# Decoding float64 weights without a limit from below: the scale moves into the ScalarE pass

## The chip, the cores and the metric

One core of one Trainium2 chip. The metric is the device time of one execution in microseconds (us). "VectorE", "ScalarE", "GpSimd", "TensorE" and "SyncE" are the core's engines; the profile writes DVE, ACT, POOL, PE and SP for them, and PEld for TensorE's weight loads. In a line of the profile, `L231` is the line of the kernel's file that issued the instruction. The same instruction has another line number in each variant of the kernel; names and shapes identify it.

## The reference

An attention block over 8 batches whose output feeds a feed-forward block:

```python
scores = scale * x @ state.T;  xread = softmax(scores) @ state
scores2 = scale * state @ x.T; sread = softmax(scores2) @ x
x = concat([xread, sread])            # 4352 rows of 512
h = x @ w_in                          # 512 x 2048
out = (h * cos(h)) @ w_out            # 2048 x 512, float32 result
```

The two weight matrices arrive as float64, because a float32 array was multiplied by a float64 scalar. The kernel computes in float32, and no engine here is given float64: it builds the float32 from the two 32-bit words of each float64.

## The kernel before

The weights come in 20 loads, mostly 128 x 1024 values each (four of the first are 128 x 512; the last two repeat part of `w_out` near the end). Each load passes through the steps below: `1` and `2` on ScalarE, `a`, `b` and `c` on VectorE (`a` of load 1 on GpSimd), and a last add on GpSimd.

```python
def convert_part(i, p):
    ...
    if p == "1":        # high word, read as a float32, without its sign
        nc.scalar.activation(dst, raw.bitcast(F32)[:, :, :, 1], func=ACTF.Abs)
    elif p == "2":      # low word -> a float32 whose lowest bits are 0 to 8
        nc.scalar.activation(e, raw.bitcast(U32)[:, :, :, 0],
                             func=ACTF.Copy, scale=2.0 ** -51, bias=2.0)
    elif p == "a":      # the limit from below
        engine = nc.gpsimd if i == 1 else nc.vector
        engine.tensor_scalar(dst, dst, 2.0 ** -15, None, op0=ALU.max)
    elif p == "b":      # shift left by 3
        nc.vector.tensor_scalar(bits, bits, 3, None, op0=ALU.logical_shift_left)
    elif p == "c":      # put the sign back
        nc.vector.scalar_tensor_tensor(out=bits, in0=raw[:, :, :, 1],
                                       scalar=-2 ** 31, in1=bits, ...)
    else:               # add the low word's part
        nc.gpsimd.tensor_tensor(bits, bits, e.bitcast(I32), op=ALU.add)
```

A float64 has 11 exponent bits and a float32 has 8. Read as a float32, the high word has the upper 8 of the 11 as its exponent and the lower 3 at the top of its fraction, so a shift by 3 brings them into place. What is left over must vanish: the float64 bias is 896 larger than the float32 one, and 896 / 8 = 112. The kernel before lets the shift and the low words' leading bits (from the bias of 2.0) take care of it, with a limit from below for tiny values.

The work is cut into steps of one tile of 128 hidden features. In each step TensorE makes a hidden product (`h`), ScalarE rounds it (`q<-h`), VectorE subtracts (`q<-q,h`, "the gate's subtraction"), ScalarE takes Abs and sine, VectorE multiplies (`g_all<-h,q`, "the gate product"), and some steps later TensorE multiplies by `w_out`. `h` has two buffers: the hidden product of a step needs the gate product of two steps earlier. In steps 0 to 14, step 9 left out, each step also converts one load. Idle matmuls of zeros (`warm(n, to)`) fill a few known holes.

## Time and profile before

| | before |
|---|---|
| time, median of 3 | 792.2 us (791.26 to 793.64) |
| span of the profiled run | 789.4 us |
| TensorE busy | 767.3 us, 97% |
| VectorE busy | 431.2 us, 55% |
| ScalarE busy | 389.3 us, 49% |
| conversions | 18 loads before 112 us, 2 at 724 to 752 us |

A share averaged over 789 us hides that the first 112 us are another regime than the rest. There VectorE and ScalarE convert weights beside the gates, and TensorE waits for them. After that TensorE is the limit.

### The profile page before, as it was taken

Reading aid. Unit: us, or ns where it says so; the run is one execution under the profiler, and the core shown is the slowest. Engines: PE = TensorE matmul, PEld = TensorE weight load, DVE = VectorE, ACT = ScalarE, POOL = GpSimd, SP = SyncE. Lnnn points to the kernel's source line nnn. Section 1 sums busy time; section 2 is a strip of 40 time slices with the busy share of each in tenths; the row PEclk is TensorE's granted clock in tenths of the full one; section 3 lists DMA queues with packets and bytes.
Section 4 is the critical chain, followed back from the end, with each engine's and each line's share of the span. In section 5 each row is a group of like instructions: output and inputs, shape, how many; then the busy total and the mean of one; then the engine's idle time right before and its main releaser. Section 6 shows DMA issues by size and latency. Waiting matters only on the chain.

```text
span 789.4 us, 7555 instructions
## 1 busy us (share of the span) xinstructions
PE 767.3 (97%) x2664; PEld 340.4 (43%) x2664; DVE 431.2 (55%) x675; ACT 389.3 (49%) x626; POOL 178.7 (23%) x119
## 2 busy tenths in 40 slices
PE   8998999899999999999999999999999999999997
PEld 3442333344344344444444434434444444455554
DVE  5879887732564467744554467635553545431531
ACT  3877964644364445643473446443563445322222
POOL 3343359684000000551000000740000004610200
PEclk9999999999999999999999999999999999999999
DMA  8485461051010610150003410340100114000021
GB/s 239 160 248 179 127 140 28 0 90 18 0 27 14 107 27 14 30 104 0 15 14 54 80 27 7 53 75 0 27 1 0 27 27 117 17 0 15 14 41 40
DMA packets 161957, 43.49 MB, mean 55 GB/s; under 512 B 153920, under 2 KB 153920, under 8 KB 161920
## 3 DMA queue, kind: packets, MB, share of 16 engines
q1 hardware_dynamic: 161024, 42.49, 24.7%
q10 hardware_dynamic: 768, 0.39, 0.2%
q8 instruction: 21, 0.34, 0.2%
q0 software_dynamic: 128, 0.13, 0.1%
q14 instruction: 16, 0.13, 0.1%
HBM read 34.08 MB, written 8.91 MB: 54 GB/s over the span
## 4 chain that ended last, share of the span: by engine, by line
PE 80%; ACT 9%; DVE 8%; issue 1%; DMA 1%; POOL 1%; SPq 0%; DVEq 0%; POOLq 0%
PE o L534 44%; PE h L469 26%; PE at L316 4%; PE o L654 3%; PE at L406 2%; DVE q L478 1%; ACT q L483 1%; ACT q L484 1%; DVE g_all L490 1%; ACT s L227 1%; ACT q L475 1%; DVE xT L336 1%; ACT xT L362 1%; DVE aT L383 1%; PE o L316 1%
## 5 line engine op out<-in xcount | busy, mean ns | idle before, releaser
L469 PE MATMUL h<-aT,sw 128*128 128x512 f32 x512 | 243.2, 598 | 10.8 <-DVE g_all L490 10.2
L534 PE MATMUL o<-g_all,w_out 128*128 128x512 f32 x512 | 236.4, 598 | 1.1 <-POOL w_out L241 1.1
L496 POOL TENSOR_TENSOR g_all<-g_all 128x512 f32<-128x512 f32 x80 | 112.1, 1424 | 450.8 <-DVE g_all L490 447.2
L475 ACT ACTIVATE q<-h 128x512 f32<-128x512 f32 (+1 forms) x144 | 82.2, 571 | 261.7 <-PE h L469 261.6
L478 DVE SCALAR_TENSOR_TENSOR q<-q,h 128x512 f32<-128x512 f32 (+1 forms) x144 | 94.2, 654 | 207.3 <-ACT q L475 207.3
L534 PE MATMUL o<-g_all,s 128*128 128x512 f32 x384 | 177.3, 598 | 0.0
L490 DVE TENSOR_TENSOR g_all<-h,q 128x512 f32<-128x512 f32 (+1 forms) x144 | 94.8, 658 | 123.9 <-ACT q L484 117.7
L469 PEld LDWEIGHTS h<-aT,sw 128*128 128x128 f32 x512 | 96.8, 191 | 136.2 <-issue 110.2
L534 PEld LDWEIGHTS o<-g_all,w_out 128*128 128x128 f32 x512 | 94.0, 190 | 125.5 <-issue 118.4
L483 ACT ACTIVATE q<-q 128x512 f32<-128x512 f32 (+1 forms) x144 | 87.6, 608 | 96.3 <-DVE q L478 96.3
L534 PEld LDWEIGHTS o<-g_all,s 128*128 128x128 f32 x384 | 70.9, 190 | 91.7 <-issue 87.3
L484 ACT ACTIVATE q<-q,halfpi 128x512 f32<-128x512 f32 (+1 forms) x144 | 100.5, 698 | 4.5
L241 POOL TENSOR_TENSOR w_out<-w_out,s 128x1024 int32<-128x1024 int32 x10 | 23.9, 2389 | 79.4 <-DVE w_out L236 79.4
L496 DVE TENSOR_TENSOR g_all<-g_all 128x512 f32<-128x512 f32 x48 | 33.2, 692 | 1.6
L443 ACT COPY sw<-at 128x512 f32<-128x512 f32 x50 | 26.8, 589 | 9.0 <-PE at L316 9.0
L469 PE MATMUL h<-sT,w_in 128*128 128x256 f32 x128 | 30.2, 379 | 0.0
L654 PE MATMUL o<-w_out,g_all 128*128 128x512 f32 x64 | 29.6, 592 | 0.0
L469 PEld LDWEIGHTS h<-sT,w_in 128*128 128x128 f32 x128 | 24.3, 190 | 10.1 <-issue 6.2
L316 PE MATMUL at<-w_in,stT 64*32 64x512 f32 x400 | 27.2, 601 | 0.0
L241 POOL TENSOR_TENSOR w_in<-w_in,s 128x1024 int32<-128x1024 int32 (+1 forms) x10 | 19.7, 1966 | 32.1 <-DVE w_in L236 18.6
L540 DVE SCALAR_TENSOR_TENSOR held<-o,held 128x512 f32<-128x512 f32 x40 | 25.3, 676 | 2.3 <-PE o L534 2.3
L561 DVE STREAM_TRANSPOSE ot<-held 128x512 f32<-128x512 f32 x32 | 22.2, 692 | 0.0
(83 smaller groups left out, 443.5 us busy)
## 6 DMA issues: line engine op xcount, KB each, us to landing
out_dram<-ot SPq DMA_DIRECT2D x132, 64.0 KB, 2.0
g_all<-in_moe_w_out_dram SPq DMA_DIRECT2D x8, 1024.0 KB, 4.9
g_all<-in_moe_w_in_dram SPq DMA_DIRECT2D x6, 1024.0 KB, 5.2
xT<-in_x_dram SPq DMA_DIRECT2D x96, 64.0 KB, 2.3
x_b<-in_x_dram SPq DMA_DIRECT2D x24, 256.0 KB, 4.7
x_b<-in_x_dram SPq DMA_DIRECT2D x16, 128.0 KB, 3.9
g_all<-in_moe_w_in_dram SPq DMA_DIRECT2D x4, 512.0 KB, 6.0
x_b<-in_moe_w_out_dram SPq DMA_DIRECT2D x1, 1024.0 KB, 6.1
```

Of the source, the lines that this page charges most:

```text
L241: nc.gpsimd.tensor_tensor(bits, bits, e.bitcast(I32), op=ALU.add)
L316: nc.tensor.matmul(out=(to or at)[j][Ns * k:Ns * k + Ns, 0:n], lhsT=w[D * j:D * j + D, self.b, Ns * k:Ns * k + Ns], rhs=r(slice(D * j, D * ...
L443: (copy or nc.scalar.copy)(sw_of[self.b, nt][:, j, c0:c1], to[j][:, 0:c1 - c0])
L469: nc.tensor.matmul(out=t.hp, lhsT=t.lhs(i), rhs=t.rhs(i), start=(i == 0), stop=(i == t.kn - 1))
L475: nc.scalar.activation(t.q, t.hp, func=ACTF.Copy, bias=MAGIC)
L478: nc.vector.scalar_tensor_tensor(out=t.q, in0=t.q, scalar=MAGIC, in1=t.hp, op0=ALU.subtract, op1=ALU.subtract)
L483: nc.scalar.activation(t.q, t.q, func=ACTF.Abs)
L484: nc.scalar.activation(t.q, t.q, func=ACTF.Sin, bias=halfpi, scale=-TWO_PI)
L490: nc.vector.tensor_tensor(t.g, t.hp, t.q, op=ALU.mult)
L496: engine.tensor_tensor(out, a, b, op=ALU.subtract)
L534: nc.tensor.matmul(out=acc[bank][ch], lhsT=w[:, i, P * ch:P * ch + P], rhs=g.g, start=(i == 0), stop=(i == NH - 1))
L654: nc.tensor.matmul(out=acc[MAIN][i], lhsT=t.g[:, P * i:P * i + P], rhs=w_out[:, :, t.f, :], start=(t.n_th == 0), stop=(t.n_th == NF - 1))
```

## The change

The intent: have the exponent corrected by a multiplication that the ScalarE pass can do anyway, so that no limit is needed and VectorE loses one pass over the weights. The low words become plain integers 0 to 8.

```diff
         if p == "1":
             nc.scalar.activation(dst, raw.bitcast(F32)[:, :, :, 1],
-                                 func=ACTF.Abs)
+                                 func=ACTF.Abs, scale=2.0 ** -112)
         elif p == "2":
             nc.scalar.activation(e, raw.bitcast(U32)[:, :, :, 0],
-                                 func=ACTF.Copy, scale=2.0 ** -51, bias=2.0)
-        elif p == "a":
-            engine = nc.gpsimd if i == 1 else nc.vector
-            engine.tensor_scalar(dst, dst, 2.0 ** -15, None, op0=ALU.max)
+                                 func=ACTF.Copy, scale=2.0 ** -29)
...
-            nc.gpsimd.tensor_tensor(bits, bits, e.bitcast(I32), op=ALU.add)
+            nc.gpsimd.tensor_tensor(bits, bits, e, op=ALU.add)
...
-    convert(0, "12ab")
-    convert(1, "12a")
+    convert(0, "12b")
+    convert(1, "12")
...
```

The other cuts are the same: the letter `a` goes from every call, and `e` is now an int32 view.

More of the change, by code (lines that the diff above doesn't have):

```diff
@@ L222, in convert_part @@
         e = low[i % 2][:, c0:c0 + m * w].rearrange("p (m f) -> p m f", m=m)
+        e = e.bitcast(I32)
         if p == "1":
             nc.scalar.activation(dst, raw.bitcast(F32)[:, :, :, 1],
-                                 func=ACTF.Abs)
+                                 func=ACTF.Abs, scale=2.0 ** -112)
         elif p == "2":
             nc.scalar.activation(e, raw.bitcast(U32)[:, :, :, 0],
-                                 func=ACTF.Copy, scale=2.0 ** -51, bias=2.0)
-        elif p == "a":
-            engine = nc.gpsimd if i == 1 else nc.vector
-            engine.tensor_scalar(dst, dst, 2.0 ** -15, None, op0=ALU.max)
+                                 func=ACTF.Copy, scale=2.0 ** -29)
         elif p == "b":
@@ L740 @@
     a0.exp2()
-    convert(2, "abcdf")
-    convert(3, "a")
+    convert(2, "bcdf")
     def plan(b):
@@ L860 @@
             convert(3, "bcdf")
-            convert(4, "1a")
+            convert(4, "1")
             go(0)
@@ L877 @@
             elif last >= 0:
-                convert(last, "abcdf")
+                convert(last, "bcdf")
             if conv >= 0 and not todo[1]:
```

## The prediction

> **What bounds the kernel now.** I read the page's busy times first, then stretches of time by engine, then who makes TensorE wait, then the timeline around the removed instruction.
>
> ```profile
> PE 767.3 (97%) x2664; PEld 340.4 (43%) x2664; DVE 431.2 (55%) x675; ACT 389.3 (49%) x626; POOL 178.7 (23%) x119
> ```
>
> TensorE is busy 97% of the span of 789.4 us. Only 22.1 us of the span are not matmul, so no change on another engine can win more than that. The stretches say where they lie (columns: length, then busy us and count of PE, PEld, DVE, ACT, POOL, then clock, DMA share, GB/s):
>
> ```profile
> 0.00:20.00 20.00, 16.82 (x60) 7.47 (x60) 11.47 (x20) 7.25 (x10) 6.61 (x13) 1.00 0.85 236
> 60.00:80.00 20.00, 15.39 (x60) 5.70 (x60) 18.37 (x26) 15.90 (x23) 7.52 (x4) 1.00 0.47 160
> 80.00:84.00 4.00, 3.91 (x12) 1.36 (x20) 2.49 (x6) 3.97 (x7) 1.94 (x1) 0.58 0.82 262
> 160.00:724.00 564.00, 562.59 (x1896) 245.19 (x1895) 286.12 (x454) 259.15 (x424) 94.24 (x66) 1.00 0.19 34
> 724.00:752.00 28.00, 28.00 (x82) 15.39 (x81) 12.49 (x21) 9.14 (x18) 4.99 (x2) 1.00 0.12 19
> ```
>
> From 160 us on TensorE has no hole worth having. The weights are converted in the first 112 us (18 loads) and again at 724 to 752 us (2 loads), where TensorE is full. So the case is decided before 112 us. TensorE's waits from 20 to 112 us:
>
> ```profile
> PE h L469 <- DVE g_all L490: 6.0, 5, 2.7
> PE o L534 <- POOL w_out L241: 1.1, 1, 1.1
> PE o L316 <- DVE stT L148: 1.1, 1, 1.1
> PE o L316 <- POOL w_in L241: 0.9, 3, 0.6
> ```
>
> With two more of 0.5 (both for ScalarE copies) that is 10.1 us. What the change touches is the limit from below (L231):
>
> ```profile
> L231 DVE TENSOR_SCALAR w_out<-w_out 128x1024 f32<-128x1024 f32 x10 | 9.3, 928 | 0.0
> L231 DVE TENSOR_SCALAR w_in<-w_in 128x1024 f32<-128x1024 f32 x6 | 4.5, 749 | 0.0
> L231 DVE TENSOR_SCALAR w_in<-w_in 128x512 f32<-128x512 f32 x3 | 1.3, 423 | 0.7 <-ACT w_in L224 0.7
> L231 POOL TENSOR_SCALAR w_in<-w_in 128x512 f32<-128x512 f32 x1 | 1.5, 1486 | 8.3 <-ACT w_in L224 8.3
> ```
>
> and this piece of timeline (start, length):
>
> ```profile
> 106.64 2.35 POOL L241 TENSOR_TENSOR w_out<-w_out,s 128x1024 int32<-128x1024 int32 x1 [3.22 <-DVE w_out L236]
> 107.28 1.98 PE L469 MATMUL h<-aT,sw 128*128 128x512 f32 x4 [1.78 <-DVE g_all L490]
> 107.73 1.82 DVE L231 TENSOR_SCALAR w_out<-w_out 128x1024 f32<-128x1024 f32 x1
> 109.59 0.69 DVE L233 TENSOR_SCALAR w_out<-w_out 128x1024 int32<-128x1024 int32 x1
> ```
>
> An undisturbed 1024-wide limit is 0.69 us, as is the shift after it. The one at 107.73 lasts 1.82: GpSimd's add ends at 108.99 and the limit 0.56 after it. The same 0.55 after the add's end shows at 52.82, 92.52 and 97.75. So the mean of 928 ns is part work, part wait for GpSimd, and the wait won't go with the instruction.
>
> **What the Trainium skill says.** "SBUF — State Buffer", section "Who interferes with whom": a VectorE operation in a 2-port mode and a GpSimd one share a pair of ports; the one that issues first keeps it, the other fully blocks. The four pairs above agree. "VectorE: DVE Perf Modes", section "Mode 2×_2P — use both read ports for one tensor": a single-source tensor_scalar gets two elements a cycle even in fp32, one with a second tensor does not. The trace agrees: 694 ns for limit and shift, 1226 ns for the sign step (L236), all 1024 wide. So the shift inherits the wait. "ScalarE: Activation LUTs", section "Step-by-step: what each stage is for": scale and bias come ahead of the function as one fused multiply-add. The trace agrees that they are free: Abs without scale is 1163 ns, Copy with scale and bias 1152. An integer output of this pass no run here has shown yet. "TensorE: Matmul & The Clock Gate", section "What's actually happening": the clock halves after an idle window. It happened once, after the 2.67 us wait before 80.09: the 4 matmul records there take 3.61 us where 1.88 to 1.98 is usual, at a clock of 0.58.
>
> **The change part by part.** Removed: 19 limits on VectorE, 9.3 + 4.5 + 1.3 = 15.1 us, and one on GpSimd, 1.5 us. Changed at equal cost: 20 Abs passes get a scale, 20 passes over the low words give integers. The order of instructions is otherwise the same on every engine (I compared the built orders: VectorE 19 fewer, GpSimd 1 fewer, nothing moved). TensorE's own work is unchanged.
>
> I followed the chain of waits from 10 to 107 us and moved each piece by what is gone ahead of it, stopping where another engine gates.
>
> 1. Start. High words (10.03) -> limit 10.87, 0.43 -> shift -> first reduction -> softmax -> GpSimd's add 19.25 -> products on TensorE 20.57. The limit is on it: 0.43. TensorE's warming matmuls end at 20.01 (11.16 + 8.85), so 0.56 could be taken, and scores end at 11.24, just before the reduction could start at 11.3. Gain 0.43.
> 2. Fourth load. GpSimd's add at 27.14 took 1.58 where others of its size take 1.27 to 1.33, beside a limit at 26.92, and the shift ahead of it waited 0.17 for an add. The wait of 0.20 it makes at 28.78 goes. Gain 0.2, together 0.6.
> 3. Sixth load. The add of 39.01 to 41.37 starts 0.14 after the sign step of its load ends (37.64 + 1.23), as all others do; the page names a ScalarE pass there, which belongs to the next load. A limit at 36.19 is ahead of it, 0.72. But TensorE is busy until 41.23 and waits only 0.19. Gain 0.2, together 0.8.
> 4. 42.5 to 57.4 us. The chain is ScalarE back to back; it is freed by those products and shortened by nothing. The seventh load's add would come 0.7 earlier and the wait of 1.15 at 46.52 shrink, but TensorE only waits later instead. Gain 0.
> 5. 57.4 to 75.5 us, VectorE. Limits at 58.03, 65.36 and 70.28 are on the chain, 0.82 + 0.65 + 0.80 with waits. By the adds moved earlier none of the three shifts that follow meets one. The first brings the state's copy (61.45) 0.87 forward. After the second, the gate's subtraction (68.52) meets ScalarE's result at 67.5, so 0.98 counts. The third gives 0.84. Gain 1.82.
> 6. 75.5 to 84.7 us, ScalarE (exp, sine, two table loads): keeps the 1.82, adds nothing. TensorE's wait of 2.67 becomes about 1.9 as it is ahead too.
> 7. 84.7 to 92.6 us, VectorE: the limit at 88.14 gives 0.73, but the subtraction at 91.93 then waits for ScalarE's result (91.65 - 1.82), so 2.10 is kept.
> 8. 92.6 to 102 us, ScalarE: 2.10 kept. The 1.35 and 1.17 us limits are beside it. In the first case the shift will meet an add (88.4 to 90.8, moved) and wait for it 0.3.
> 9. 102 to 107.3 us, VectorE: the limit at 103.82, 0.72 with its spacing. The last wait of TensorE, 107.28, comes 2.10 + 0.73 = 2.83 forward; its wait shrinks from 1.78 to about 1.5.
>
> Sum 0.8 + 2.8 = 3.6 us. After 112 us TensorE sets the pace and carries the 3.6 to the end. Its three waits at 150, 156 and 327 us come from softmax steps of a later batch and should move along unchanged; the two limits at 730.77 and 744.52 are worth nothing. So 792.2 - 3.6 = 788.6 us.
>
> **The rivals.**
> A. Hidden entirely: VectorE is only 55% busy and TensorE 97%, so nothing, 791.5 to 792.5 us. Against it: VectorE is 18.37 of 20 us busy from 60 to 80 us, and TensorE waits there by name for VectorE.
> B. All 15.1 us count, 777 us. Against it: TensorE waits only 10.1 us in the stretch that holds 18 of the conversions, ScalarE is as full (14.72 of 16 us from 44 to 60), and what of the 15.1 is port wait goes to the shift. Even with every such wait gone and the 1.7 us of halved clock, an end of 792.2 - 11.8 = 780.4 is a gain of 1.5%.
> C. The shift takes over the port waits and ScalarE's chain takes over the rest sooner than I think: 1 to 2 us of gain, 790 to 791. For it: ScalarE has only 7.4 us of waits for VectorE from 20 to 112 us, 3.3 of them in one place.
> D. ScalarE's integer output is slower. Were it 0.5 us on each of 20 passes, an estimate without a row behind it, 18 of them would lengthen ScalarE's stretches by up to 9 us and the end by perhaps 4: 794 to 797. Against it: changing the type on the input side (uint32) already costs nothing.
> E. TensorE's wait near 77.5 gets short enough that the clock doesn't halve: 1.7 us of TensorE time, but TensorE then waits for VectorE at 91 and 107 us instead, so at most a few tenths.
>
> **Range and chances.** My chain carries 20 hand-offs, each good to 0.05 to 0.1, and C is the likeliest error, so I keep more room above than below the centre: 786.8 to 790.8 us. The runs of before spread over 2.4 us (791.26 to 793.64), which is within that. 2% is 15.8 us; TensorE's holes in reach (11.8) don't hold it, and D would need some 40 us of new work. Faster by over 2%: 0.01, within 2%: 0.98, slower by over 2%: 0.01.
>
> **What would show it.** VectorE's busy time falls by some 13 to 14 us rather than 15.1, the shift's mean at 1024 wide rising above 694 ns wherever an add runs beside it. TensorE's busy time stays at 767 or, if the clock stays up at 80 us, falls to 765.6. The wait at 20.57 nearly vanishes, the one at 80 us shrinks to about 1.9, that at 107 us is about 1.5 and begins near 104.4. ScalarE's two passes keep 1.15 us; a longer integer pass would mean D. I am wrong if the first products don't start near 20.1, if TensorE passes its last wait before 112 us less than 2 or more than 5 us earlier, or if a wait beyond 112 us grows and gives the gain back.

## The result, and the profile after

| | before | after |
|---|---|---|
| time, median of 6 | 791.51 us (791.21 to 793.64) | 787.01 us (786.81 to 788.56) |
| ratio | | 0.9941 (95% interval 0.9928 to 0.9954) |
| span of the profiled run | 789.4 us | 785.0 us |

A ratio is the mean time of one kernel's runs over that of the other's of the same rounds, so it isn't quite the ratio of the medians. The gain is 4.5 us of the medians, 0.6%: within 2%, and clear of the noise.

The busy times of the changed kernel:

```profile
PE 765.1 (97%) x2664; PEld 340.3 (43%) x2664; DVE 417.3 (53%) x656; ACT 389.1 (50%) x626; POOL 176.7 (23%) x118
```

VectorE lost 431.2 - 417.3 = 13.9 us in 19 instructions, ScalarE nothing. The groups of instructions say that the removed 15.1 us came back in part. The shift, now alone (columns: count, busy us, mean ns):

```profile
L231 DVE TENSOR_SCALAR w_out<-w_out 128x1024 int32<-128x1024 int32 x10 | 8.2, 822 | 0.0
L231 DVE TENSOR_SCALAR w_in<-w_in 128x1024 int32<-128x1024 int32 x6 | 4.0, 674 | 0.0
```

Its mean over `w_out` was 694 ns. The extra comes from two places. This is the larger one, in the changed kernel's timeline, with TensorE's last wait before 112 us between its two lines:

```profile
102.36 2.36 POOL L239 TENSOR_TENSOR w_out<-w_out,s 128x1024 int32<-128x1024 int32 x1 [3.67 <-ACT q L473]
...
102.99 1.98 PE L467 MATMUL h<-aT,sw 128*128 128x512 f32 x4 [1.21 <-DVE g_all L488]
103.45 1.82 DVE L231 TENSOR_SCALAR w_out<-w_out 128x1024 int32<-128x1024 int32 x1
```

The add ends at 104.72 and the shift 0.55 later, at 105.27. It is the picture that the prediction shows for the limit, with the shift in the limit's place. The other one, at 89.02, took 0.90.

The stretches of the changed kernel that answer to those of before (length, busy us and count of PE, PEld, DVE, ACT, POOL, clock, DMA share, GB/s):

```profile
60.00:80.00 20.00, 18.05 (x81) 6.86 (x78) 16.25 (x25) 17.58 (x26) 8.22 (x4) 1.00 0.60 209
80.00:84.00 4.00, 1.57 (x5) 0.50 (x4) 2.90 (x5) 3.97 (x7) 0.00 (x0) 1.00 0.00 0
160.00:724.00 564.00, 562.59 (x1896) 245.41 (x1896) 286.19 (x453) 260.29 (x425) 89.94 (x63) 1.00 0.19 34
```

TensorE was busy 18.05 instead of 15.39 us from 60 to 80 us, ScalarE 17.58 instead of 15.90, with VectorE less busy. The stretches are fixed in time while the work moved forward through them, so their edges count: the wait of 2.67 us before 80.09 fell into the first stretch, and the one of 2.43 us that stands there now falls into the second. From 160 to 724 us TensorE's busy time is the same. TensorE's waits from 20 to 112 us, after:

```profile
PE h L467 <- DVE g_all L488: 3.8, 3, 1.9
PE h L467 <- ACT sw L441: 2.9, 2, 2.4
PE o L532 <- POOL w_out L239: 1.2, 1, 1.2
...
PE o L314 <- DVE stT L148: 0.3, 1, 0.3
```

The wait for the gate product fell from 6.0 to 3.8 us and the wait for the adds of `w_in` is gone from TensorE's row (its weight loads still wait for them, 1.5 us instead of 3.2); a wait for ScalarE's copies (`sw`) of 2.4 us is new. To see how the 4.5 us add up, it is better to follow single events. The table gives the start of the same event in both traces. The two executions did not start alike: the first score products stand at 9.60 and 9.53 us, before anything that the change touches, so 0.07 is taken from each difference.

| event | before | after | earlier by | predicted |
|---|---|---|---|---|
| first products of the weights (TensorE) | 20.57 | 20.10 | 0.40 | 0.43 |
| gate product of step 1 (VectorE) | 32.86 | 32.20 | 0.59 | 0.6 |
| copy of the second products (ScalarE) | 42.53 | 41.14 | 1.32 | 0.8 |
| gate's subtraction of step 6 | 57.43 | 56.07 | 1.29 | 0.8 |
| gate's subtraction of step 9 | 74.78 | 71.51 | 3.20 | 2.6 |
| gate's subtraction of step 12 | 91.93 | 88.41 | 3.45 | 2.9 |
| TensorE's last wait before 112 us | 107.28 | 102.99 | 4.22 | 3.6 |
| TensorE's wait at 150 us | 150.43 | 146.14 | 4.22 | 3.6 |

Only one row adds an error: between 33 and 43 us the change gained 0.73 and 0.2 had been predicted. All later rows carry those 0.5 along. Here are the lines of that place, the timelines of TensorE (PE) and of its weight loads (PEld) before and after (start, length; `x8` are eight small matmuls or their weight loads). The last line is from a later place of the changed kernel:

```profile
40.17 1.06 PE L316 MATMUL o<-w_in,stT 64*32 64x512 f32 x8
41.42 1.06 PE L316 MATMUL o<-w_in,stT 64*32 64x512 f32 x8 [0.19 <-POOL w_in L241]
...
41.42 0.15 PEld L316 LDWEIGHTS o<-w_in,stT 64*32 64x32 f32 x8 [1.10 <-POOL w_in L241]
```

```profile
39.51 1.57 PE L314 MATMUL o<-w_in,stT 64*32 64x512 f32 x16
...
40.02 0.15 PEld L314 LDWEIGHTS o<-w_in,stT 64*32 64x32 f32 x8 [0.36 <-POOL w_in L239]
...
89.67 1.09 PE L314 MATMUL o<-w_in,stT 64*32 64x512 f32 x16
```

The second eight products need a converted load, and in both kernels they follow GpSimd's add of that load. Before, the add ends at 41.37 (39.01 + 2.36) and their weight loads start at 41.42; after, it ends at 39.97 (37.61 + 2.36) and they start at 40.02. In all fourteen traces they start 0.05 to 0.06 after that add. So this add, and the limit ahead of it, are on the chain in full: the add ends 1.33 earlier, which is the 0.59 of the row above and the 0.7 of one limit.

TensorE's own row shows only 0.19 of this wait, because it counts TensorE as busy with the first eight until 41.23. That was no bar to the second eight. After the change they start at 40.02, while the first eight last until 40.57 (39.51 + 1.06). Sixteen whose operands are ready take 1.09 us (last line), 0.03 more than eight alone. The 1.57 us of the `x16` still hold a wait for the add; there is only no hole in which the row could show it. The row of the weight loads shows the difference: 1.10 us of waiting before and 0.36 after, 0.74 less.

### The profile page after: what moved, and what is told of

It is laid out like the page before. It is cut to its first block, busy times and chain, and to the rows that moved or that the text cites. A ratio compares the mean times of both kernels' runs of the same rounds, so it can differ in the third digit from the quotient of the medians.

```text
span 785.0 us, 7535 instructions
## 1 busy us (share of the span) xinstructions
PE 765.1 (97%) x2664; PEld 340.3 (43%) x2664; DVE 417.3 (53%) x656; ACT 389.1 (50%) x626; POOL 176.7 (23%) x118
## 4 chain that ended last, share of the span: by engine, by line
PE 81%; ACT 10%; DVE 6%; issue 1%; DMA 1%; SPq 0%; POOL 0%; DVEq 0%
PE o L532 44%; PE h L467 26%; PE at L314 4%; PE o L652 4%; PE at L404 2%; ACT q L482 1%; ACT q L481 1%; ACT s L228 1%; DVE q L476 1%; ACT q L473 1%; DVE g_all L488 1%; ACT xT L360 1%; ACT w_in L225 1%; ACT L482 1%; DVE xT L334 1%
## 5 line engine op out<-in xcount | busy, mean ns | idle before, releaser
L559 DVE STREAM_TRANSPOSE ot<-held 128x512 f32<-128x512 f32 x32 | 22.1, 692 | 0.0
```

## The experiments

All but one start from the changed kernel. In the first seven the limit comes back as a maximum with 0, which leaves every value as it is (they are all positive after Abs), on the same engine and at the same place, for a chosen set of loads:

```diff
+BACK = {...}          # which loads
...
+        elif p == "a":
+            if i in BACK:
+                engine = nc.gpsimd if i == 1 else nc.vector
+                engine.tensor_scalar(dst, dst, 0.0, None, op0=ALU.max)
...
-    convert(0, "12b")
+    convert(0, "12ab")       # and so on: the letter a again at its 20 places
```

All twelve gave the reference's result. Theory 1 is the prediction's: the gain is the removed limits on the chain of waits, and where another engine gates, a limit is worth nothing. The rivals are that the new number format changes ScalarE's passes, that every removed limit counts alike, and that TensorE's clock, halved near 80 us before and not after, made the gain.

The changed kernel was not timed again beside these runs. The kernel before, which was, took 791.51, 791.68 and 791.84 us in the three sets of rounds (the second set on another chip), and the 95% interval of each ratio is about 1 us wide on either side. A cost under 1 us can't be told from the times alone, then; it rests on the traces, where a start that came later is taken off. A trace shows one run, and single runs of one kernel lie up to 2.4 us apart.

**All 20 limits back.** `BACK` is all loads. The order of VectorE's and GpSimd's instructions is then that of the kernel before; only the format is new.

> The changed number format with all 20 limits put back (a maximum with 0, which leaves the values as they are, same engines, same places: the order of instructions is that of the kernel before). Theory 1 (the gain is the removed limits on the chain of waits, the format costs nothing): 791.5 us within 0.4, last TensorE wait before 112 us again near 107.3, VectorE busy again near 431. Rival D (scaled Abs and integer output change the ScalarE passes): differs from 791.5 by over 0.8 us in either direction.

Measured: 791.46 us (791.22 to 791.9, 5 runs), before in the same rounds 791.51, ratio 0.9999 (0.9985 to 1.0012); VectorE busy 431.1 us, TensorE's last wait at 107.44. Less the start, later by 0.10, the last wait is 0.06 from that of the kernel before. The format costs and gains nothing that shows, and the 4.5 us are the limits.

**Limits of loads 0 to 4 back.** `BACK = {0, 1, 2, 3, 4}`.

> The changed kernel with the limits of loads 0 to 4 only put back. Theory 1: the copy of the gate product now at 32.20 us comes at about 32.9 (0.66 later), the end 787.0 + 0.7 = 787.7 us. If load 5's step meets the products later too, up to 788.0. Rival A (start hidden): 787.0. Rival of equal shares (4.5 us over 20 limits): 5 of 20, 788.1.

Measured: 787.81 us (787.57 to 788.2), 0.8 above the changed kernel's 787.01. The gate product of step 1 stands at 32.94, TensorE's last wait at 103.79; less the 0.13 by which this execution's first score products were later (9.66 against 9.53), that is 0.61 and 0.67 later than in the changed kernel. By the trace, as theory 1 has it and not as equal shares do (5 of 20 of the 4.22 in the table would be 1.06); the times alone, 787.57 to 788.2, don't exclude the 788.1 of equal shares.

**Limit of load 5 back.** `BACK = {5}`.

> The changed kernel with the limit of load 5 only put back. Prediction's own term (TensorE's shown wait, 0.2): 787.2 us. Theory 1 as corrected from the two traces (a stream of 16 products split in two ends 0.7 later, though the profile shows a wait of only 0.15 to 0.2): ScalarE's copy of the products at 41.8 instead of 41.14, end 787.7 us, shown wait before the second eight products at most 0.3. Equal shares: 787.2.

Measured: 787.63 us (787.57 to 789.06), 0.6 more. ScalarE's copy stands at 41.97. Its timeline shows the later add and the second eight products behind it:

```profile
38.45 2.35 POOL L244 TENSOR_TENSOR w_in<-w_in,s 128x1024 int32<-128x1024 int32 x1 [3.55 <-ACT s L229]
...
39.61 1.06 PE L319 MATMUL o<-w_in,stT 64*32 64x512 f32 x8
...
40.86 1.06 PE L319 MATMUL o<-w_in,stT 64*32 64x512 f32 x8 [0.18 <-POOL w_in L244]
```

One limit of 0.69 us, a shown wait of 0.18, and 0.6 us at the end of the kernel. This is the term that the prediction had at 0.2. The expectation had the size right, but its reason, that a stream is split in two, was not: the add ends at 40.80, and the second eight's weight loads start at 40.86, 0.06 after it as everywhere.

**Limits of loads 9, 10, 11, 13 and 16 back.** `BACK = {9, 10, 11, 13, 16}`.

> The changed kernel with the limits of loads 9, 10, 11, 13 and 16 only put back, the five that the prediction put on the chain between 57 and 107 us. Theory 1: 787.0 + 2.9 = 789.9 us within 0.5, last TensorE wait near 105.9. Equal shares: 788.1. Rival clock (1.7 us came from the TensorE clock not halving near 80 us): the cost is 1.7 if and only if the matmuls near 80 us run at half clock again.

Measured: 790.37 us (790.15 to 791.33), 3.4 more, where 2.9 was expected within 0.5. The trace accounts for the size: TensorE's last wait before 112 us is at 106.27; less a later start of 0.54 (first score products at 10.07) it is 2.74 later than after the change, close to the 2.83 that the prediction gave these loads. The rest of this run came beyond 112 us, after a wait that every variant has:

```profile
149.43 3.61 PE L472 MATMUL h<-aT,sw 128*128 128x512 f32 x4 [1.86 <-DVE g_all L493]
```

The four take 1.98 in the changed kernel after the same wait of 1.86. Here the clock was halved, where TensorE is the limit. Whether the later start and this made up the 0.5 in the four untraced runs too can't be told. Near 80 us the matmuls ran at full clock (1.98 at 78.35, after a wait of 1.95), so the 1.7 us of the clock rival had no part in the cost. Five limits carry two thirds of the gain.

**Nine limits that the prediction left off the chain back.** `BACK = {6, 7, 8, 12, 14, 15, 17, 18, 19}`.

> The changed kernel with the limits of loads 6, 7, 8, 12, 14, 15, 17, 18 and 19 only put back, nine that the prediction left off the chain. Theory 1: 787.0 us, at most 0.4 more (load 14's shift meets an add, load 8's add comes later and can hold the shift of load 9 by 0.13). Equal shares: 9 of 20 of 4.5, 789.0. Rival B (every limit counts its 0.7): 793.

Measured: 788.14 us (787.45 to 789.66): 1.1 more, where at most 0.4 was expected. A miss. In the trace the whole loss lies between 46 and 52 us:

```profile
43.66 2.37 POOL L244 TENSOR_TENSOR w_out<-w_out,s 128x1024 int32<-128x1024 int32 x1 [3.45 <-ACT w_in L226]
...
46.09 2.68 PE L537 MATMUL o<-g_all,w_out 128*128 128x512 f32 x4 [1.87 <-POOL w_out L244]
...
48.56 2.92 PE L472 MATMUL h<-aT,sw 128*128 128x512 f32 x4
...
51.52 0.60 ACT L478 ACTIVATE q<-h 128x512 f32<-128x512 f32 x1 [1.00 <-PE h L472]
```

The add of load 6 comes 0.7 later, TensorE waits 1.87 for it instead of 1.16, and its next eight matmul records take 2.68 and 2.92 instead of 1.88 to 1.98: the clock from 44 to 50 us was 0.77. ScalarE, which is the chain there, then waits 1.00 for the hidden product. Two more runs took this apart.

**Limit of load 6 alone, and the other eight without it.**

> The changed kernel with the limit of load 6 only put back. Reading of the run with nine limits back: load 6 delays an add by 0.7, TensorE's wait near 46 us grows from 1.16 to 1.87, and in some runs its clock then halves to 51 us, which makes ScalarE wait 1.0 for a hidden product. So: 787.0 in most runs, some near 788.1, and a halved clock near 46 us in the trace only if the profiled run is a long one. Rival (a limit anywhere costs some tenths): 787.4 in all runs.

> The changed kernel with the limits of loads 7, 8, 12, 14, 15, 17, 18 and 19 put back, without load 6. Same reading: 787.0 to 787.3, last TensorE wait before 112 us near 103.0 as in the changed kernel. Rival (a limit anywhere costs some tenths, 8 of 20): 788.0.

Measured: load 6 alone 787.5 us, its five runs 786.84, 787.23, 787.5, 788.16 and 788.52, so only two near 787.0 where most were expected; the profiled one was the run of 788.16, and it has the halved clock that was expected for such a run (matmuls at 46.15 take 3.31, and ScalarE waits 1.04). The eight others: 787.21 us (787.0 to 789.05), the profiled run of 787.0 with TensorE's last wait at 103.21, or 0.07 later than in the changed kernel after a start 0.15 later. So eight limits, 5.5 us of VectorE work at 0.69 each, cost about nothing in the traced run. The two traces were not of like runs: one was among the longest of its five, the other the shortest. The means of the five, 787.65 and 787.64 us, don't tell the two kernels apart, and the changed kernel itself had one run of 788.56. What the trace shows for load 6 is that with its limit back TensorE's wait grows to 1.89 and its clock can halve there; how much that costs on average stays open, and so does what made the long untraced runs long.

**The clock near 80 us.** The kernel before, with two idle matmuls in the hole of 2.67 us:

```diff
+        if step == 11:
+            warm(2, acc[SIDE][1])
         if step != 1:
             hidden(t)
```

> The kernel before with two idle matmuls of zeros put on TensorE ahead of the hidden product of step 11, in the hole of 2.67 us before 80.09. Rival clock (halved clock after that hole costs the kernel before 1.7 us, and the change saved that): 789.8 us, matmuls at 80 us at 1.9 instead of 3.6 us. Theory 1 (TensorE waits for VectorE again at 91 and 107 us, so its speed at 80 isn't on the chain): 791.5 within 0.3, though the matmuls at 80 us are at full clock.

Measured: 791.28 us (791.17 to 791.76), before in the same rounds 791.68, ratio 0.9994 (0.9982 to 1.0007). The clock did stay up, as the timeline shows:

```profile
80.22 1.98 PE L469 MATMUL h<-aT,sw 128*128 128x512 f32 x4 [0.96 <-DVE g_all L490]
86.83 1.98 PE L469 MATMUL h<-aT,sw 128*128 128x512 f32 x4 [1.69 <-ACT sw L443]
91.62 1.98 PE L469 MATMUL h<-aT,sw 128*128 128x512 f32 x4 [0.22 <-DVE g_all L490]
107.47 1.98 PE L469 MATMUL h<-aT,sw 128*128 128x512 f32 x4 [1.82 <-DVE g_all L490]
```

The four matmul records at 80 us take 1.98 instead of 3.61. TensorE then waits 1.69 at 86.83, where it had not waited before, and meets VectorE at 91.62 and 107.47 with the same waits as without the idle matmuls (0.20 and 1.78). So the 1.7 us that TensorE lost at half clock were never on the chain, and the clock rival falls.

**A faster kernel from the freed VectorE.** From 42 to 57 us and from 88 to 98 us ScalarE sets the pace while VectorE has room. The first attempt moves one of the four copies of the second batch's turned tokens to VectorE (the expectation says "two", meaning none but this one: it is one), the second moves the two copies of that batch's first products as well:

```diff
-                pairs(s[0], b, "tokens", "tokens_kept", 0)
-                pairs(s[1], b, "tokens", "tokens_kept", 2)
+                for k in range(NK):
+                    pe[s[k // 2]].append((b, "tokens", k))
+                x_act[s[0]].append((b, "tokens_kept", 0))
+                y_dve[s[0]].append((b, "tokens_taken", 1))   # nc.vector.tensor_copy
+                x_act[s[1]].append((b, "tokens_kept", 2))
+                y_act[s[1]].append((b, "tokens_kept", 3))
...
-            if b == 1 and nt > 0:                            # second attempt only
+            if b == 1:
```

> An attempt at a faster kernel: the changed kernel with two of the four copies of the second batch's turned tokens moved from ScalarE to VectorE (the second and, of the same step, no other: the second pair stays). Theory 1 with ScalarE as the chain from 41 to 57 us: ScalarE is freed of one copy of 0.47 there, end 786.6 us. Rival (VectorE or TensorE gates there): 787.0 or more.

> The same, and the two copies of the second batch's first products (near 93.5 us) moved from ScalarE to VectorE. Theory 1 with ScalarE as the chain from 88 to 98 us: about 0.5 us less again, 786.1 us. Rival (the copies push the next shift and sign step on VectorE by 1.2 us and the gate product with them): 786.6 to 787.5.

Measured: 786.38 us (786.34 to 787.26), ratio to before 0.9934; and 786.57 us (785.83 to 787.94), ratio 0.9934. The first is as expected: TensorE's wait near 146 us stands at 146.01, or 0.49 earlier than in the changed kernel once its start, later by 0.36, is taken off. The second, expected at 786.1, is no faster than the first by its median, and spreads over 2.1 us. In its trace TensorE was at half clock after a wait of 2.43 at 83.47, and ScalarE waited for hidden products later (0.20 at 97.15, 0.68 at 101.81). The last pair adds idle matmuls to both:

```diff
+        if step in (11, 12):
+            warm(step - 10, acc[SIDE][1])
```

> The changed kernel with one copy of turned tokens on VectorE, and three idle matmuls of zeros in TensorE's two holes near 76 and 83 us, so that its clock stays up. If the halved clock there costs the end nothing in most runs: 786.4 as without them. If it costs in some: the runs come closer together, 786.3 in all.

> The same with the two copies of the second batch's first products on VectorE too. In the trace without the idle matmuls the clock was halved near 83 us and ScalarE then waited for TensorE at 97 and 102 us. With the clock up: 785.9 in all runs, the fastest of this study. Rival (VectorE's 1.2 us of copies gate): 786.4.

Measured: 787.11 us (786.56 to 788.23) for the first, no better than without and spread as widely: a miss. Its profiled run of 787.88 had no halved clock near 80 us, but a late start (the first hidden product at 22.53 instead of 21.28) and a halved clock at 147 us. For the second 786.11 us (785.71 to 787.16), ratio to before 0.9931 (0.9918 to 0.9945), with the clock up at both holes. Three of its five runs lie within 0.2 of the expected 785.9, the others at 786.81 and 787.16. In its profiled run, of 785.71, the waits stand like this:

```profile
102.12 1.98 PE L470 MATMUL h<-aT,sw 128*128 128x512 f32 x4 [0.69 <-DVE g_all L491]
145.27 1.98 PE L470 MATMUL h<-aT,sw 128*128 128x512 f32 x4 [1.86 <-DVE g_all L491]
```

That is 0.87 earlier than the changed kernel's 146.14, or 0.97 with its start 0.10 later. It is the lowest median, but it and the changed kernel were not timed in the same rounds and the intervals of their ratios overlap, so the order rests on the two traces. That the idle matmuls narrow the spread is not shown: 1.5 us against 2.1 in one pair, 1.7 against 0.9 in the other.

## Why the prediction was right

It gave 788.6 us, in a range of 786.8 to 790.8, and 787.0 was measured: right, at the low end of the range. It counted from 792.2, the median of the first three runs of the kernel before; the six gave 791.51, so 0.7 of the 1.6 us between 788.6 and 787.0 is the starting point. The gain was put at 3.6 and was 4.5. By its steps:

1. Start: 0.43 predicted, 0.40 seen; with the limits of loads 0 to 4 back the last wait is 0.67 later, against 0.6 for steps 1 and 2 together.
2. Fourth load: 0.6 together, 0.59 seen. The copies behind the products moved as predicted.
3. Sixth load (load 5): the term that was mis-sized. The prediction took TensorE as busy until 41.23 and so its shown wait, 0.19, as the most that could be won. But what stood on TensorE was no bar to the products that waited; they follow the add by 0.05, and the limit of 0.72 ahead of it counted in full. It was worth 0.73 in the traces and 0.6 in the run that put it back.
4. ScalarE's stretch to 57.4 us: nothing, as seen. But the statement that the wait at 46.52 would shrink was wrong. It stayed at 1.16, since TensorE too arrived earlier, by the gain of step 3. And calling load 6 free held only in part: with the others gone, its limit pushes TensorE to where the clock can halve.
5. VectorE's stretch to 75.5 us: 1.82 predicted, 3.20 - 1.29 = 1.91 seen.
6. ScalarE's stretch to 84.7 us: the gate product behind it kept the gain (84.68 to 81.45, 3.16). The wait of 2.67 became 1.95, with 1.9 predicted. What was not foreseen is the new wait of 2.43 at 83.45: at full clock TensorE was ready early there. It cost nothing.
7. VectorE to 92.6 us: 2.10 kept was predicted, 3.45 - 1.29 = 2.16 seen.
8. ScalarE to 102 us: the shift that would meet an add met it, 0.2 instead of 0.3 us.
9. To 107.3 us: 2.83 predicted, 4.22 - 1.29 = 2.93 seen; the wait left is 1.21, not 1.5.

The waits at 150 and 156 us moved along unchanged, 1.86 and 0.97 before and after within 0.01. VectorE's busy time fell by 13.9, within the predicted 13 to 14, and the shift did take over port waits. TensorE's busy time, foreseen at 767 or 765.6, was 765.1, so the 22.1 us outside it were no strict limit, as the prediction had called them; it rests on the same reading of a busy TensorE as step 3. Rival A (hidden) and B (all of it) fall with the time. D falls with the format run. E was right that this wins nothing; the idle matmuls showed it. That the clock near 80 us did not halve was in part luck: after the same wait of 1.95 it did in the run with load 5's limit back. C, the likeliest error as the prediction had it, pointed the wrong way: the gain was larger, not smaller.

One more thing the runs showed that no step had. Against 787.01, the four groups that together are all 20 limits (loads 0 to 4, load 5, the five, the nine) cost 0.8, 0.6, 3.4 and 1.1 when put back one group at a time, 5.9 in sum, but 4.5 all together. Part of the excess is no limit at all (the 0.5 us of the five's run that its trace puts beyond 112 us, and the halved clock in the nine's). By the traces, the last wait before 112 us comes 0.67, 0.62 and 2.74 later for the first three groups, 4.03 in sum, and 4.28 for all 20; so most of the excess lies in the group of nine and beyond 112 us. That limits on parallel branches hide each other, load 6 behind load 5, fits the traces and wasn't tested by a pair of its own.

## What to carry to other kernels

Before counting a removed instruction, follow what waited for it: in the traces eight limits were worth about nothing and five two thirds of the gain. A wait that TensorE's row shows before a group of small matmuls can be far less than what the group waited, because the row counts the group before it as busy while the later one could already run beside it. Read the row of the weight loads too (1.10 where TensorE's row had 0.19), see what ends just before they start, and compare with a group whose operands were ready (1.09 us for sixteen here). After a change frees an engine, look for the copies that the new limiting engine does and the freed one could do.

## What the Trainium skill lacked or had wrong

- "TensorE: Matmul & The Clock Gate", section "What's actually happening": it has the clock halve after an idle window of about 3.4 us in a free-running pattern. Here it halved after much shorter shown waits, and not each time: after 1.86 (matmuls of 3.61 us, limits of the five back), after 1.95 (3.61, load 5 back), but not after 1.95 in the changed kernel (1.98), nor after 2.67 in the run of eight limits (1.99). That the same hole can do either agrees with a free-running window; a length of 3.4 us doesn't fit these waits.
- "TensorE: Matmul & The Clock Gate", section "Part 3: Packing small matmuls — row/col tiling": it has a model of one pack, but no figure for one whose second half is released late. Measured here at 64 x 32 tiles and 512 columns: eight alone 1.06 us, sixteen with ready operands 1.09 us, and sixteen whose second eight could start 0.51 us after the first eight 1.57 us.
- No page that I read tells the cost of an integer output on ScalarE. A 128 x 1024 pass from uint32 to int32, which reads every second word, took 1.11 to 1.17 us, as the one to float32 did (1.15 in the mean).
